# q and k of the first eight attention tiles loaded two tokens to a run and turned by products with the identity

## The chip, the cores and the metric

The kernel runs on one core of a Trainium2 chip. Its time is the device time of one execution: 847.76 us, the median of 3 runs (847.44 to 847.93). The core has a matrix engine (PE, with its weight loads PEld beside it), a vector engine (DVE), a scalar engine (ACT), GpSimd (POOL) and SyncE (SP), which here only issues DMAs.

## The reference

Three stages follow each other. Attention runs within chunks of 64 tokens: 4 batches x 8 heads x 576 tokens x 64. Its output, 2304 tokens x 512, goes through two layers of the same shape (512 to 2048 to 512) with different functions in the middle.

```python
scores = scale * np.matmul(q_c, k_c.transpose(0, 1, 2, 4, 3))   # 64 x 64 per chunk and head
scores = scores - np.max(scores, axis=-1, keepdims=True)
attn = np.exp(scores)
attn = attn / (np.sum(attn, axis=-1, keepdims=True) + 1e-09)
out = np.matmul(attn, v_c)
...
x = np.ascontiguousarray(attn_out.transpose(0, 2, 1, 3)).reshape(B * S, H * D)
h = x @ w_in                                                    # first layer
g = np.maximum(h, 0.0) + np.log1p(np.exp(-np.abs(h)))
x = g @ w_out
h = x @ w_in                                                    # second layer
g = P(h) / (Q(h) + 1e-6)                                        # two small polynomials
return g @ w_out
```

## The kernel before

**Tiles and blocks.** Attention works on 18 tiles of 128 tokens, two chunks each. The first layer takes tokens in blocks: three of 512 (blocks 0, 1, 2), then two of 384 that are computed as a pair. A block goes through 16 steps, one per 128 columns of the hidden layer. A step has 12 products `h` (L1065), two functions on ACT (`t` L1132 and `g` L1137), a subtraction on DVE that splits `g` in two parts (L1140), and 12 products `acc` (L1646). The 24 products of a step are 128x512. The second layer does the same with five blocks, the lines L1576 to L1608 and `acc` at L1679.

**Attention of a tile.** q and k are brought to a layout with the head dimension on the partitions (`qkT`), then come 16 products for the scores (L729, or L716), maximum, subtraction, exponential, sum and division on DVE and ACT (the division on POOL for tiles 7 to 17), the weights are turned (`aT`), 16 products with v (L857, or L845) follow, and the result is split into `xT`, an operand of the first layer.

**Two ways to turn.** The tiles in `STAGED` (0 to 6) turn q and k on PE, 4 transposes of 128x128 for q and 4 for k (`transpose`, L677), which ACT copies out of PSUM (`take`, L689); their attention weights are turned on PE too (L816, copied at L838). Tiles 7 to 17 turn on DVE, in blocks of 32x32: q and k at L701 and the weights in 8 instructions at L829. Their loads place such blocks where the DVE wants them, which takes 8 DMAs for q and 8 for k (`load_qk`, L618) and 4 for v (L633). A staged tile takes one DMA for q and one for k (L609; two where a batch ends inside the tile).

**What sets the order.** The kernel first lists tasks with an engine, a cost in us and what they read and write (`add`). A planner (`Program.schedule`) then simulates these costs with many random orders and keeps the one that ends first, and the program is written out in that order on every engine. For tiles 7 to 17 the planner counts 2.8 us for the q loads, 2.8 us for the k loads and 1.4 us for v. `BEGUN` and `BEGIN_AT` say how many tiles, and at which steps of blocks 0, 1 and 2, join the list of tasks. The wait for PE in the first microseconds is filled with products that compute nothing (`warm`, L1982).

**Buffers.** Loads of weights (`wr_1i`, `wr_2o`, ...) and of q and k of tiles 7 to 17 share 4 `raw` buffers. Weights arrive as 64-bit numbers and are put together in `cm_` tiles (3 buffers, tag `m`): ACT starts one (L468, L470), DVE finishes it (L474, L483). In blocks 1 and 2 the weights of the second layer are prepared in this way and stored back to DRAM (`store`, L523), and a `cm_` buffer is free when that store has landed. The results `h` have two PSUM buffers.

Of the kernel before, what the change touches and what calls it, by code (L numbers as in the profile page):

```python
# [11 lines left out]
F32 = mybir.dt.float32  # L12
# [8 lines left out]
P = 128  # L21
CH = 64
# [17 lines left out]
APART = (0, 3)  # L40
NP = 384
PIECES = ((0, 256), (256, 256))
STAGED = tuple(range(7))
LAST_FINISH = 12
LEAD = 0.0
LEAD2 = 0.0
BEGUN = (1, 5, 5)
BEGIN_AT = ((9,), (0, 3, 6, 9, 13), (0, 2, 4, 7, 9))
CONVERT = ((), (1, 2, 4, 5, 7, 8, 10, 11, 12, 14, 15), (1, 2, 3, 4, 5))
BACK = (0, 0, 1, *(1,) * 13)  # L50
QK_BY_VECTOR = {*range(18)} - {*STAGED}
# [251 lines left out]
def tile_chunk_attention_two_ffn(  # L303
# [276 lines left out]
    def attention(tb, scored_too=None):  # L580
# [14 lines left out]
        def chunks():  # L595
            for c in range(2):
                b, s = divmod(tb * TB + c * CH, S)
                yield c, b, s

        def load_qk(n):  # L600

            def f():
                if not staged and n == 0:
                    qk_t[tb] = raw.tile([P, 2, H, D], F32, tag="raw", name=f"qk_{tb}")
                if not qk_by_vector:
                    for off, m, b, s in runs(tb * TB, TB):
                        sync.dma_start(  # L609
                            out=qk_t[tb][off : off + m, n],  # L610
                            in_=(q, k)[n][b, :, s : s + m, :].rearrange("h p d -> p h d"),
                        )
                    return
                for c, b, s in chunks():
                    for d0 in range(0, D, 32):
                        for t0 in range(0, CH, 32):
                            p0 = CH * c + d0
                            sync.dma_start(  # L618
                                out=qk_t[tb][p0 : p0 + 32, n, :, t0 : t0 + 32],
                                in_=(q, k)[n][  # L620
                                    b, :, s + t0 : s + t0 + 32, d0 : d0 + 32
                                ].rearrange("h p d -> p h d"),
                            )

            return f

# [45 lines left out]
        def transpose(n):  # L672
            def f():
                if n == 0:
                    new_ps()
                for g in range(4):
                    pe.transpose(  # L677
                        bank(n)[:, g * P : (g + 1) * P],
                        qk_t[tb][:, n, 2 * g : 2 * g + 2].rearrange("p h d -> p (h d)"),
                        ident,  # L680
                    )

            return f

        def take(n):
            def f():
                if n == 0:
                    new_turned()
                act.activation(  # L689
                    tiles["qkT"][:, n].rearrange("p g t -> p (g t)"), bank(n), AF.Copy  # L690
                )

            return f
# [203 lines left out]
        km, ks = turn("mx", 4), turn("sm", 4)  # L897
        turned = [("turned", name, n) for n in range(16)]
        kr = [[(room_key[tb, n], h) for h in range(2)] if first else [] for n in range(2)]
        for n in range(2):  # L900
            loads["qk"[n], tb] = add(
                DMA, 2.8 if qk_by_vector else 1.2, load_qk(n), [],
                [(qkey, n)] if n else [qkey, (qkey, 0), (qkey, 1)],
                alloc=None if staged or n else "raw",
            )
        qks = [qkey, (qkey, 0), (qkey, 1)]
        if chained:

            def transposes():
                for n in range(2):  # L910
                    transpose(n)()

            begin[tb, 0] = add(PE, 0.9, transposes, qks, [b0, b1], alloc=alloc)
            for n in range(2):
                add(
                    ACT, 0.48, take(n), [(b0, b1)[n]], turned[8:] if n else turned,
                    alloc=None if n else "qkT",
                )
        elif not qk_by_vector:
            for n in range(2):  # L920
                begin[tb, n] = add(
                    PE, 0.46, transpose(n), [qkey, (qkey, n)], [(b0, b1)[n]] if n else [b0, b1],
                    alloc=None if n else alloc,
                )
                add(
                    ACT, 0.48, take(n), [(b0, b1)[n]],
                    turned[8 * n : 8 * n + 8] if n else turned + kr[0],
                    alloc=None if first or n else "qkT",
                )
        else:  # L930
            for n in range(2):
                add(
                    DVE, 0.6, turn_blocks(n), [qkey, (qkey, n)], turned[8:] if n else turned,
                    alloc=None if n else "qkT",
                )
        if not by_chunk:
# [3 lines left out]
        else:  # L940
            if not finish_attention(scores, turned):
                add(PE, 0.78, scores, turned, [b0, b1], alloc=alloc)
            add(DMA, 1.4, load_v, [], [(vkey, 0)], alloc="v")
        if scored_too:
            scored_too()
        if apart:
# [1012 lines left out]
    with tc.manual_schedule():  # L1959
# [2 lines left out]
        vec.memset(far_t, -FAR)  # L1962
        table(EXP_LN)
        for tb in STAGED:
            qk_t[tb] = wpool.tile([P, 2, H, D], F32, tag="wi", name=f"qk_{tb}")
        for fc in range(FC - len(STAGED)):
            wts[1, "i", fc] = new_w((1, "i", fc))
        for tb in STARTING:
# [59 lines left out]
```

## Time and profile before

| | us |
|---|---|
| median of 3 runs | 847.76 |
| the profiled execution | 849.12 |
| its span, first to last instruction | 847.3 |
| PE busy | 829.0 (98%) |
| DVE busy | 611.4 (72%) |
| ACT busy | 519.4 (61%) |
| POOL busy | 224.2 (26%) |

The profiled execution is 1.36 us above the median, and 1.82 us of it lie outside the span. A busy table gives for a stretch of the span each engine's busy time, the granted clock of PE as a share of 2.4 GHz, and the mean busy share of the 16 DMA engines. "x32" counts records; a product of two 4-byte operands (`warm`, scores, products with v) leaves two records, because PE goes over it twice, while a transpose leaves one.

### The profile page before, as it was taken

To read this page: it belongs to the slowest core of one execution; us is meant where nothing else is said; L and a number is where in the kernel's file an instruction comes from. 1 tells how busy PE (TensorE), PEld (TensorE's weight loads), DVE (VectorE), ACT (ScalarE), POOL (GpSimd) and SP (SyncE) were. 2 spreads that over 40 slices of the span, in tenths; PEclk is the share of its full clock that TensorE was granted. 3 is DMA by queue.
4 is the path that set the end of the run, shared out by engine and by line. 5 is a ranking of instruction groups with operands and counts; after the bars stand their busy time and mean duration, and the time that the engine had idled before them with its cause. 6 is when DMAs were issued, how large, how long until landed. Compare 5 with 4: busy or idle time off the path is not lost.

```text
span 847.3 us, 13413 instructions
## 1 busy us (share of the span) xinstructions
PE 829.0 (98%) x4978; PEld 706.7 (83%) x4978; DVE 611.4 (72%) x1080; ACT 519.4 (61%) x927; POOL 224.2 (26%) x205
## 2 busy tenths in 40 slices
PE   7999999999998899999999999999999999999998
PEld 6788878878877689999998888888889888888886
DVE  5778874675663668555379988778688886778775
ACT  5799863333321345555548788657678876667674
POOL 0000002242221241111111398332225262222131
PEclk9899999999999899999999999999999999999999
DMA  9975644655464101000383343010022000001001
GB/s 221 233 231 156 201 113 131 172 156 119 99 181 98 59 4 50 1 1 1 127 258 96 92 125 87 19 45 1 0 54 97 1 26 1 0 9 42 1 0 51
DMA packets 114722, 71.14 MB, mean 84 GB/s; under 512 B 84192, under 2 KB 102112, under 8 KB 114656
## 3 DMA queue, kind: packets, MB, share of 16 engines
q1 hardware_dynamic: 114656, 70.28, 30.4%
q8 instruction: 39, 0.64, 0.3%
q14 instruction: 27, 0.22, 0.1%
HBM read 56.63 MB, written 13.63 MB: 83 GB/s over the span
## 4 chain that ended last, share of the span: by engine, by line
PE 86%; DVE 4%; DMA 4%; ACT 2%; SPq 2%; issue 1%; POOL 0%; ACTq 0%; POOLq 0%; DVEq 0%
PE h L1065 34%; PE acc L1679 23%; PE acc L1646 20%; PE u L1453 3%; PE p L1453 3%; SPq L618 1%; DMA wr_1o<-in_moe_w_out_dram 1%; DMA wr_2i<-in_moe_w_in_dram 1%; PE warm L1982 1%; DMA qk<-in_k_dram 1%; DMA qk<-in_q_dram 1%; PE aps L845 1%; PE aps L677 1%; SPq L633 1%; DVE t L1553 0%
## 5 line engine op out<-in xcount | busy, mean ns | idle before, releaser
L1065 PE MATMUL h<-xT,w_2i 128*128 128x512 f32 (+1 forms) x960 | 208.7, 368 | 0.0
L1679 PE MATMUL acc<-w_2o,g 128*128 128x512 f32 x864 | 207.7, 390 | 0.1
L1065 PEld LDWEIGHTS h<-xT,w_2i 128*128 128x128 f32 x960 | 169.0, 188 | 31.4 <-ACT u L1576 0.3
L1679 PEld LDWEIGHTS acc<-w_2o,g 128*128 128x128 f32 x864 | 161.1, 188 | 33.7 <-POOL g L1583 0.9
L1646 PE MATMUL acc<-g,w_1o 128*128 128x512 f32 (+1 forms) x768 | 177.9, 378 | 1.6 <-ACT g L1137 0.8
L1646 PEld LDWEIGHTS acc<-g,w_1o 128*128 128x128 f32 x768 | 140.5, 188 | 25.0 <-DVE g L1140 1.5
L1583 POOL TENSOR_TENSOR g<-t,g 128x512 fp32r<-128x512 f32 (+1 forms) x80 | 95.5, 1195 | 232.4 <-ACT g L1580 181.0
L1065 PE MATMUL h<-xT,w_1i 128*128 128x512 f32 x564 | 137.4, 395 | 7.3 <-ACT g L1137 7.3
L1065 PEld LDWEIGHTS h<-xT,w_1i 128*128 128x128 f32 x564 | 106.3, 190 | 30.6 <-ACT g L1137 8.3
L1608 DVE TENSOR_TENSOR t<-h,t 128x512 f32<-128x512 f32 (+1 forms) x80 | 50.9, 636 | 31.8 <-ACT t L1568 12.9
L1597 ACT ACTIVATE t<-h,row 128x512 f32<-128x512 f32 (+1 forms) x80 | 58.7, 733 | 24.3 <-PE h L1065 23.8
L1140 POOL TENSOR_TENSOR g<-t,g 128x512 fp32r<-128x512 f32 x32 | 43.2, 1350 | 103.0 <-ACT g L1137 101.8
L1553 DVE SCALAR_TENSOR_TENSOR t<-t,row,u 128x512 f32<-128x512 f32 (+1 forms) x80 | 55.2, 691 | 19.6 <-ACT u L1576 19.0
L1572 ACT ACTIVATE u<-t,row 128x512 f32<-128x512 f32 (+1 forms) x80 | 51.8, 648 | 25.0 <-DVE t L1553 24.3
L1553 DVE SCALAR_TENSOR_TENSOR t<-t,row,h 128x512 f32<-128x512 f32 (+1 forms) x80 | 55.3, 692 | 12.9 <-ACT u L1550 5.7
L1580 ACT ACTIVATE g<-t 128x512 fp32r<-128x512 f32 (+1 forms) x80 | 46.8, 585 | 27.6 <-DVE t L1553 23.7
L1568 ACT ACTIVATE t<-h,row 128x512 f32<-128x512 f32 (+1 forms) x80 | 51.2, 642 | 17.1 <-PE h L1065 9.8
L1553 DVE SCALAR_TENSOR_TENSOR t<-u,row,t 128x512 f32<-128x512 f32 (+1 forms) x80 | 55.3, 693 | 6.0 <-ACT u L1550 5.8
L1553 DVE SCALAR_TENSOR_TENSOR u<-t,row,u 128x512 f32<-128x512 f32 (+1 forms) x80 | 55.5, 695 | 0.0
L1132 ACT ACTIVATE t<-h 128x512 f32<-128x512 f32 x48 | 28.4, 594 | 42.7 <-PE h L1065 41.8
L809 POOL TENSOR_TENSOR e<-e,sm 128x512 f32<-128x512 f32 x11 | 12.6, 1144 | 152.6 <-DVE sm L805 147.9
L1550 ACT ACTIVATE u<-h 128x512 f32<-128x512 f32 (+1 forms) x80 | 43.3, 542 | 14.9 <-DVE t L1608 9.7
(157 smaller groups left out, 1037.3 us busy)
## 6 DMA issues: line engine op xcount, KB each, us to landing
wr_1i<-in_moe_w_in_dram SPq DMA_DIRECT2D x16, 512.0 KB, 5.0
wr_1o<-in_moe_w_out_dram SPq DMA_DIRECT2D x16, 512.0 KB, 5.0
wr_2i<-in_moe_w_in_dram SPq DMA_DIRECT2D x16, 512.0 KB, 4.7
wr_2o<-in_moe_w_out_dram SPq DMA_DIRECT2D x16, 512.0 KB, 5.1
out_dram<-ev SPq DMA_DIRECT2D x16, 256.0 KB, 2.1
x<-ev SPq DMA_DIRECT2D x6, 512.0 KB, 2.7
x2r<-x SPq DMA_DIRECT2D x6, 512.0 KB, 4.6
qk<-in_q_dram SPq DMA_DIRECT2D x88, 32.0 KB, 3.0
```

What stands on the lines that cost most here:

```text
L1065: pe.matmul(hs[s], w[:, a, c * P : (c + 1) * P], xt[:, b, c, :n_tok], start=n == 0, stop=n == 3 * KC - 1,)
L1453: pe.matmul(banks[n], lhs(a, i, c), right(b, j, c), start=start and m == 0, stop=m == 5, skip_group_check=not start,)
L1550: act.activation(u(), h(), AF.Square)
L1553: return lambda: vec.scalar_tensor_tensor(out=out(), in0=in0(), scalar=scalar, in1=in1(), op0=op0, op1=op1)
L1568: act.activation(new("t1"), h(), AF.Abs, scale=b_t[:, 0:1])
L1572: act.activation(u(), d(), AF.Ln, bias=epsq_t)
L1580: act.activation(gs[s][:, 0, :n_tok], p(), AF.Copy)
L1583: pool.tensor_tensor(out=gs[s][:, 1, :n_tok], in0=p(), in1=gs[s][:, 0, :n_tok].bitcast(F32), op=ALU.subtract,)
L1597: lambda: act.activation(new("t2"), h(), AF.Identity, scale=na_t[:, 3:4], bias=na_t[:, 2:3]),
L1608: lambda: vec.tensor_tensor(out=p(), in0=h(), in1=p(), op=ALU.mult), [hkey, kp], [kp],
L1646: pe.matmul(accs[1, j, half][c % 2][:, :n_tok], wts[1, "o", fc][:, a, c * P : (c + 1) * P], gs[s][:, b, :n_tok], start=first and n == 0, s ...
L1679: pe.matmul(accs[2, j, half][c % 2], gs[s][:, b, c * P : (c + 1) * P], wts[2, "o", fc][:, a, :], start=first and n == 0, stop=last and n == 2,
```

## The change

Tile 7 becomes a staged tile, so that eight tiles turn q and k on PE. A staged tile now keeps q on partitions 0 to 63 and k on 64 to 127, with two neighbouring tokens of a head side by side: runs of 512 bytes in DRAM where runs of 256 bytes were read. Since a partition holds two tokens, the 4 + 4 transposes become 8 products for the even tokens and 8 for the odd ones: 128 rows by 64 columns of data stand in PE, the identity's 128 columns pass through, and the results go by turns to the lower and the upper half of the PSUM partitions. Both sets need q and k. ACT's copy out of PSUM puts even and odd tokens back in order.

For the other ten tiles the 16 DMAs of q and k stay as they are, but are listed as eight tasks of two DMAs at 0.95 us each; v counts 2.0 us. Five tiles joined the list in block 1 and five in block 2, one in block 0; now six and four, and none in block 0.

```diff
-STAGED = tuple(range(7))
+STAGED = tuple(range(8))
...
-BEGUN = (1, 5, 5)
-BEGIN_AT = ((9,), (0, 3, 6, 9, 13), (0, 2, 4, 7, 9))
+BEGUN = (0, 6, 4)
+BEGIN_AT = ((), (0, 3, 6, 9, 11, 14), (0, 3, 6, 9))
...
+        def load_part(n, c, d0):
+            def f():
+                if (n, c, d0) == (0, 0, 0):
+                    qk_t[tb] = raw.tile([P, 2, H, D], F32, tag="raw", name=f"qk_{tb}")
+                b, s = divmod(tb * TB + c * CH, S)
+                p0 = CH * c + d0
+                for t0 in range(0, CH, 32):
+                    sync.dma_start(
+                        out=qk_t[tb][p0 : p0 + 32, n, :, t0 : t0 + 32],
+                        in_=(q, k)[n][b, :, s + t0 : s + t0 + 32, d0 : d0 + 32].rearrange(
+                            "h p d -> p h d"
+                        ),
+                    )
...
         def load_qk(n):
...
+                for off, m, b, s in runs(tb * TB, TB):
+                    p0 = CH * n + off // 2
+                    sync.dma_start(
+                        out=qk_t[tb][p0 : p0 + m // 2].rearrange("p h t d -> p h (t d)"),
+                        in_=(q, k)[n][b, :, s : s + m, :].rearrange(
+                            "h (p t) d -> p h (t d)", t=2
+                        ),
+                    )
...
-                for g in range(4):
-                    pe.transpose(
-                        bank(n)[:, g * P : (g + 1) * P],
-                        qk_t[tb][:, n, 2 * g : 2 * g + 2].rearrange("p h d -> p (h d)"),
-                        ident,
+                for h in range(H):
+                    p0, col = 64 * (h % 2), h // 2 * P
+                    pe.matmul(
+                        bank(n)[p0 : p0 + 64, col : col + P], qk_t[tb][:, h, n], ident,
+                        start=True, stop=True,
                     )
...
                 act.activation(
-                    tiles["qkT"][:, n].rearrange("p g t -> p (g t)"), bank(n), AF.Copy
+                    tiles["qkT"].rearrange("p n g (u t) -> p t g n u", t=2)[:, n],
+                    bank(n).rearrange("p (g n u) -> p g n u", g=4, n=2),
+                    AF.Copy,
                 )
...
-            loads["qk"[n], tb] = add(
-                DMA, 2.8 if qk_by_vector else 1.2, load_qk(n), [],
-                [(qkey, n)] if n else [qkey, (qkey, 0), (qkey, 1)],
-                alloc=None if staged or n else "raw",
-            )
+            if staged:
+                loads["qk"[n], tb] = add(
+                    DMA, 1.0, load_qk(n), [], [(qkey, n)] if n else [qkey, (qkey, 0), (qkey, 1)]
+                )
+                continue
+            for part_key in loaded_parts[n]:
+                begins = part_key == loaded_parts[0][0]
+                loads["qk"[n], tb] = add(
+                    DMA, 0.95, load_part(*part_key[1:]), [],
+                    [qkey, *loaded_parts[0], *loaded_parts[1]] if begins else [part_key],
+                    alloc="raw" if begins else None,
+                )
...
-                    PE, 0.46, transpose(n), [qkey, (qkey, n)], [(b0, b1)[n]] if n else [b0, b1],
+                    PE, 0.46, transpose(n), qks, [(b0, b1)[n]] if n else [b0, b1],
...
-            add(DMA, 1.4, load_v, [], [(vkey, 0)], alloc="v")
+            add(DMA, 2.0, load_v, [], [(vkey, 0)], alloc="v")
```

The order of the program changes on every engine, since the planner starts anew. Three places follow, before and then after. Names end in a running number that grows with the place in the program.

**SyncE in the middle of block 2.** Before: the last two tiles' loads (`qk_2803`, `qk_2860`) and the stores `w2o` and `w2i` of prepared weights.

```order
L618 DMA qk_2803<-in_q_dram 32x8x32 x8
L618 DMA qk_2803<-in_k_dram 32x8x32 x8
L618 DMA qk_2860<-in_q_dram 32x8x32 x8
L633 DMA v_2912<-in_v_dram 64x4x64 x4
L618 DMA qk_2860<-in_k_dram 32x8x32 x8
L523 DMA w2o_2959<-cm_2o_2528 128x512
L523 DMA w2i_2967<-cm_2i_2683 128x512
```

After, the same place, with the last two tiles `qk_2883` and `qk_2989`:

```order
L607 DMA qk_2883<-in_q_dram 32x8x32 x6
L607 DMA qk_2883<-in_k_dram 32x8x32 x2
L607 DMA qk_2883<-in_q_dram 32x8x32 x2
L607 DMA qk_2883<-in_k_dram 32x8x32 x6
L638 DMA v_2958<-in_v_dram 64x4x64 x4
L523 DMA w2i_2985<-cm_2i_2728 128x512
L607 DMA qk_2989<-in_q_dram 32x8x32 x4
L607 DMA qk_2989<-in_k_dram 32x8x32 x2
L607 DMA qk_2989<-in_q_dram 32x8x32 x4
L607 DMA qk_2989<-in_k_dram 32x8x32 x6
L523 DMA w2o_3083<-cm_2o_2878 128x512
L523 DMA w2o_3087<-cm_2o_2665 128x512
```

One store has moved between the two tiles' loads, and v of the first of them stands between them as well; the store of the oldest `cm_` tile (`cm_2o_2665`; before `cm_2o_2528`) still stands behind both tiles.

**ACT at the same place.** Before, from the function `t` of step 39 on:

```order
L1132 ACTIVATE t_39_2955<-h_39_2917 128x512
L1137 ACTIVATE g_2985<-h_39_2917 128x512
L470 ACTIVATE cm_2i_2993<-wr_2i_2776 128x512
L470 ACTIVATE cm_2o_2997<-wr_2o_2791 128x512
L1132 ACTIVATE t_40_3014<-h_40_2972 128x512
L1132 ACTIVATE t_41_3026<-h_41_3000 128x512
L1137 ACTIVATE g_3071<-h_40_2972 128x512
```

After, from `t` of step 39 on:

```order
L1147 ACTIVATE t_39_2999<-h_39_2966 128x512
L1147 ACTIVATE t_40_3057<-h_40_3004 128x512
L1152 ACTIVATE g_3081<-h_39_2966 128x512
L781 ACTIVATE e_3071<-e_3071,row 128x512
L1152 ACTIVATE g_3119<-h_40_3004 128x512
L470 ACTIVATE cm_2i_3124<-wr_2i_2841 128x512
L470 ACTIVATE cm_2o_3127<-wr_2o_2844 128x512
L1051 ACTIVATE xb_3137<-aps 128x512
L1147 ACTIVATE t_41_3140<-h_41_3105 128x512
L1152 ACTIVATE g_3167<-h_41_3105 128x512
```

Before, the two conversions `cm_2i` and `cm_2o`, which take the buffers that the stores free, stand ahead of `t` and `g` of step 40. After, they stand behind both, and ahead of `t` and `g` of step 41.

**PE where the first step begins.** Before, from the turned weights of tile 1 on (`room_1_132`; 134 and 136 are tiles 2 and 3):

```order
L816 MATMUL aps_173<-ident,room_1_132 128x128 x4
L816 MATMUL aps_208<-ident,room_1_134 128x128 x4
L857 MATMUL aps_173<-room_1_132,v_138 64x64 x16
L857 MATMUL aps_208<-room_1_134,v_139 64x64 x16
L1982 MATMUL warm_407<-ident 128x128 x2
L816 MATMUL aps_0_245<-ident,room_1_136 128x128 x4
L1982 MATMUL warm_407<-ident 128x128
L1090 MATMUL h_0_421<-xT_330,w_1i_120 128x256 x4
```

After:

```order
L823 MATMUL aps_198<-ident,room_1_132 128x128 x4
L864 MATMUL aps_198<-room_1_132,v_138 64x64 x16
L823 MATMUL aps_222<-ident,room_1_134 128x128 x4
L823 MATMUL aps_0_262<-ident,room_1_136 128x128 x4
L864 MATMUL aps_222<-room_1_134,v_139 64x64 x16
L1105 MATMUL h_0_446<-xT_363,w_1i_121 128x256 x4
```

The `warm` products between the tiles are gone, and so is their place ahead of the turned weights of tile 3.

## Rows read from the trace of the kernel before

**Rows 1.** part 1 of the page: busy us (share of the span) xinstructions
```profile
PE 829.0 (98%) x4978; PEld 706.7 (83%) x4978; DVE 611.4 (72%) x1080; ACT 519.4 (61%) x927; POOL 224.2 (26%) x205
```

**Rows 2.** busy table, 300 to 400 us: length, engines, clock, DMA share, GB/s
```profile
300.00:400.00 100.00, 100.00 (x575) 95.66 (x574) 66.23 (x135) 52.84 (x116) 21.51 (x21) 1.00 0.03 11
```

**Rows 3.** the waits of PE: us in total, times, longest
```profile
PE h L1065 <- ACT g L1137: 7.3, 3, 6.0
```

**Rows 4.** PE in time order, 262 to 285 us: start, us, what [idle]
```profile
263.40 5.60 PE L1065 MATMUL h<-xT,w_1i 128*128 128x512 f32 x24
...
278.86 4.69 PE L1065 MATMUL h<-xT,w_1i 128*128 128x512 f32 x12 [6.04 <-ACT g L1137]
```

**Rows 5.** ACT in order of time, 225 to 300 us
```profile
276.08 0.66 ACT L470 ACTIVATE cm_2i<-wr_2i 128x512 f32<-128x512 f32 x1 [11.82 <-DMA w2o<-cm_2o]
```

**Rows 6.** SyncE's DMA issues in order of time, 100 to 310 us
```profile
251.13 5.29 SPq L618 DMA_DIRECT2D qk<-in_q_dram  x8
...
261.52 3.85 SPq L618 DMA_DIRECT2D qk<-in_q_dram  x8
265.47 2.58 SPq L633 DMA_DIRECT2D v<-in_v_dram  x4
268.09 4.06 SPq L618 DMA_DIRECT2D qk<-in_k_dram  x8
272.19 0.46 SPq L523 DMA_DIRECT2D w2o<-cm_2o  x1
```

**Rows 7.** chain that ended last, 40 to 62 us: start, us, what
```profile
48.06 0.62 PE aps L857 x32
48.68 0.47 PE aps L729 x32
...
58.90 0.44 PE aps L816 x4
...
60.74 0.87 PE aps L677 x8
```

**Rows 8.** the same chain, 0 to 120 us
```profile
6.55 0.45 PE warm L1982 x4
```

**Rows 9.** PE in order of time, 60 to 300 us
```profile
109.62 4.15 PE L1646 MATMUL acc<-g,w_1o 128*128 128x512 f32 x17 [0.58 <-DVE g L1140]
```

**Rows 10.** busy table, three stretches of the start
```profile
2.00:12.00 10.00, 9.81 (x119) 8.80 (x118) 2.99 (x7) 4.12 (x8) 0.00 (x0) 1.00 1.27 223
...
22.00:24.00 2.00, 1.71 (x8) 1.71 (x9) 1.99 (x5) 1.07 (x3) 0.00 (x0) 0.50 1.25 261
...
45.00:50.00 5.00, 5.00 (x83) 4.00 (x82) 3.59 (x7) 4.97 (x9) 0.00 (x0) 1.00 1.04 362
```

**Rows 11.** DVE in order of time, 0 to 50 us
```profile
8.19 0.76 DVE L754 TENSOR_REDUCE mx<-aps 128x4 f32<-128x256 f32 x2 [7.29 <-PE aps L729]
...
10.42 0.69 DVE L754 TENSOR_REDUCE mx<-aps 128x8 f32<-128x512 f32 x1 [0.82 <-PE aps L729]
...
12.65 0.69 DVE L809 TENSOR_TENSOR room<-room,sm 128x512 f32<-128x512 f32 x1
```

**Rows 12.** PE in order of time, 0 to 60 us
```profile
18.38 1.26 PE L816 MATMUL aps<-ident,room 128*128 128x128 f32 x8 [2.84 <-DVE room L809]
...
22.30 1.22 PE L1982 MATMUL warm<-ident 128*128 128x128 f32 x4 [0.59 <-DVE xT L415]
...
24.45 1.20 PE L1090 MATMUL h<-xT,w_1i 128*128 128x256 f32 x4
```

**Rows 13.** ACT by line, 24 to 112 us: count, busy, mean ns, idle
```profile
L370 ACT ACT_TABLE_LOAD x18 | 23.1, 1283 | 0.3
...
L689 ACT ACTIVATE qkT<-aps 128x512 f32<-128x512 f32 x6 | 3.6, 603 | 1.0 <-PE aps L677 1.0
```

**Rows 14.** busy table, 40 to 112 us
```profile
40.00:80.00 40.00, 39.66 (x333) 32.13 (x333) 32.37 (x61) 38.62 (x60) 0.00 (x0) 1.00 0.61 174
80.00:112.00 32.00, 31.42 (x167) 25.34 (x166) 27.89 (x52) 28.06 (x41) 1.04 (x1) 1.00 0.71 223
```

More of the change, by code (lines that the diff above doesn't have):

```diff
@@ L598, in chunks @@
                 yield c, b, s
+        def load_part(n, c, d0):
[11 more added lines that the diff above has]
+                    )
+            return f
         def load_qk(n):
             def f():
[L605 to L611, printed above, removed]
-                        )
[L613 to L623, printed above, removed]
+                for off, m, b, s in runs(tb * TB, TB):
[6 more added lines that the diff above has]
+                    )
             return f
@@ L899, in attention @@
         kr = [[(room_key[tb, n], h) for h in range(2)] if first else [] for n in range(2)]
+        loaded_parts = [[(qkey, n, c, d0) for c in range(2) for d0 in (0, 32)] for n in range(2)]
         for n in range(2):
-            loads["qk"[n], tb] = add(
-                DMA, 2.8 if qk_by_vector else 1.2, load_qk(n), [],
-                [(qkey, n)] if n else [qkey, (qkey, 0), (qkey, 1)],
-                alloc=None if staged or n else "raw",
-            )
+            if staged:
[10 more added lines that the diff above has]
+                )
         qks = [qkey, (qkey, 0), (qkey, 1)]
@@ L932, in attention @@
                 add(
-                    DVE, 0.6, turn_blocks(n), [qkey, (qkey, n)], turned[8:] if n else turned,
+                    DVE, 0.6, turn_blocks(n), [qkey, *loaded_parts[n]], turned[8:] if n else turned,
                     alloc=None if n else "qkT",
@@ L1964, in tile_chunk_attention_two_ffn @@
         for tb in STAGED:
-            qk_t[tb] = wpool.tile([P, 2, H, D], F32, tag="wi", name=f"qk_{tb}")
+            qk_t[tb] = wpool.tile([P, H, 2, D], F32, tag="wi", name=f"qk_{tb}")
         for fc in range(FC - len(STAGED)):
```

## The prediction

> **What bounds the kernel now.** I read the busy times first: PE works 829.0 of 847.3 us [rows 1]. Then the busy table by stretches: behind 300 us PE has no gap to give back [rows 2], so whatever this change wins or loses is won or lost in the first 300 us, and every microsecond of work added to PE there shows in full unless it falls into a gap. Third, the waits of PE: 7.3 us in three waits for one function of ACT [rows 3]. In order of time, 6.04 us of it is a single gap in block 2, and the 12 products behind it took 4.69 us, while 24 took 5.60 just before [rows 4]; beside 5.60 / 2 = 2.8 that is 1.9 us more, since PE came back at the lower clock. The place costs 7.9 us. Fourth, what ACT waited for there: 11.82 us ahead of a conversion of weights, for a store of an older tile [rows 5]. Fifth, why the store was late: SyncE issued the q and k loads of two tiles and a v load ahead of it [rows 6], 21.1 us from the first (251.13) to the store (272.19). So this wait is a queue on SyncE, not a lack of bandwidth. The rest of the gaps are small, apart from the start, where PE waits for the tiles' softmax on DVE.
>
> **The change part by part.** The sum is made against the profiled execution, 849.12 us, which is 1.36 us above the median 847.76; I carry the difference over to the median.
>
> *The queue of block 2.* One tile's 16 loads of q and k take SyncE 3.85 + 4.06 = 7.9 us, and v 2.58 [rows 6], 10.5 together. The planner counted 2.8 + 2.8 + 1.4 = 7.0, so behind two tiles and one v it took the stores for 2 x 2.3 + 1.2 = 5.8 us earlier than they were. It now counts 8 x 0.95 + 2.0 = 9.6. In the new order the oldest conversion tile's store still stands behind two tiles' loads, so SyncE needs some 2 x 7.9 + 2.58 + a store = 19 us there, not much less than 21.1. What differs is who is queued behind the wait: on ACT the two conversions moved from ahead of the functions of step 40 to behind them. PE then has a further step of 24 products (2 x 2.8 = 5.6 us, by the products of [rows 4]) plus the scores and values of a tile (0.47 + 0.62 [rows 7]) = 6.7 us before it needs what ACT holds back. That covers the 6.04 us even if the stores come as late as before, and SyncE has 2 us less to do. Term: -7.9. If the loads start later than before by more than about 2.7 us (6.7 - 6.04 + 2), the difference comes back; bounds -7.9 and 0.
>
> *Turning on PE.* A transposed tile costs 0.87 us in 8 transposes [rows 7]. The new 16 products pass 128 columns over PE twice. The nearest row by columns is the warm product: 0.45 us for four passes, 0.11 each [rows 8]. One after another 32 passes are 3.6 us; if the lower and the upper half run side by side, 1.8. Products on a part of the array do overlap in this trace: the scores make 32 passes of half as many columns, 32 x 0.056 = 1.8 us one by one, in 0.47 us, 3.8 at a time; those with v in 0.62, 2.9 at a time [rows 7]. Four at a time cannot come from different rows of the array alone, so two column halves can run together. With v, where neighbours in the queue change the column half first, as here, each 32 passes cost 0.62 - 1.8/4 = 0.17 us above the ideal; 1.8 + 0.17 gives 2.0 us per tile, the value I take, between 1.8 and 3.6. Tiles 4, 5 and 6 lie on PE's full stretch: 3 x (2.0 - 0.87) = +3.4 (2.8 to 8.2). Tile 7 had cost PE nothing for turning; now 2.0 for q and k and 0.44 for its weights [rows 7]: +2.4 (2.2 to 4.0).
>
> The Trainium skill ("TensorE: Matmul & The Clock Gate", Part 3, What overlaps and what doesn't) says that a weight load overlaps products in flight only when it goes to another row group. Here all products use all rows, so by that rule each of the loads would stand bare. By it the price would lie towards the upper bound above; the scores row, in which two column halves share rows, speaks against the strict reading, and no row shows 128 rows by 64 columns.
>
> *Relief on DVE.* Tile 7 loses two transposes and eight small ones on DVE at about 100 us, where PE waited 0.58 us for DVE [rows 9]. Term: -0.6, between -0.6 and 0.
>
> *The start.* Tiles 0 to 3 also turn with 2.0 instead of 0.87 us, in a stretch where PE waits for data anyway: in 2 to 12 us the loads came at 223 GB/s with the DMA engines full [rows 10]. In 45 to 50 us, with weights in longer runs under way, it was 362 GB/s [rows 10]; 512-byte runs lie between, and if a packet has a fixed cost, they give 1 / (1/362 + (1/223 - 1/362)/2) = 276 GB/s. Four tiles' q and k are 2.1 MB: 9.4 us before, 7.6 us after, so the last tile's data is some 1.8 us earlier (0 to 3.6). But nothing can be turned now before k has come. Behind k's arrival stood 0.44 us of turning and now stand 2.0; a quarter of the 1.8 us is won, so tile 0's scores come 2.0 - 0.44 - 0.45 = 1.1 us later, and DVE begins at 9.3 instead of 8.19 [rows 11]. The scores of tile 1 stand behind the turning of tiles 1 and 2: 9.3 + 4.0 + 0.5 = 13.8 instead of 10.42. Until then DVE can finish the sum and the division of tile 0, 0.69 each by the row of the division [rows 11], which came later before: 3.4 - 1.4 = 2 us later in all. Against it: the weights of tiles 1 and 2 were turned after a gap of 2.84 us, then two warm products held PE, 0.59 us of waiting and 1.22 of work at the clock 0.50, ahead of tile 3, and the first step began at 24.45 [rows 10, 12]. Those two are gone in the new order. Two later, two earlier: term 0, between -2 (the clock holds, since the gap is shorter) and +6 (four tiles at 3.6 us: (3.6 - 2.0) x 4 = 6.4).
>
> *ACT and the loads in block 0.* ACT gets three copies more (two of q and k, one of the weights, 0.60 each) and two table loads more in block 0 (1.28 each [rows 13]): 4.4 us. It was busy 38.62 of 40 us up to 80 and 28.06 of 32 up to 112 [rows 14], so 5.3 us were free, and PE's 5.8 us of added work lengthen the block as much. Tile 7's loads are earlier too, into the time of full DMA. I take +0.5 for new short waits, between 0 and 3. The interleaved order of ACT's copy has no row; at the double of 0.60 it would be 0.6 x 16 = 9.6 us of ACT work, of which four tiles lie in the block; the data is read in runs of 64, so I count nothing.
>
> Sum: -7.9 + 3.4 + 2.4 - 0.6 + 0 + 0.5 = -2.2. The profiled execution would take 846.9, the median 847.76 - 2.2 = 845.6 us.
>
> **The rivals.** *The two halves do not run side by side* (slower). Place: the 16 products of each staged tile. At 3.6 us a tile, tiles 4 to 7 cost 8.2 + 3.2 + 0.4 = 11.8 us instead of 5.8, and the first step starts 6 us later: 845.6 + 6.0 + 6.0 = 857.6. The scores row speaks against it. The change turns to a loss where a tile costs more than 2.0 + 2.2 / 4 = 2.55 us even with an unchanged start.
>
> *The wait of block 2 stays or comes back elsewhere* (slower). Ten tiles still pass SyncE in two blocks, six of them in block 1, which had five; a late store again holds ACT. For it: the oldest store stands behind two tiles as before. Against: the planner's costs now fit the measured ones to 10%. With three quarters of the 7.9 us lost, 845.6 + 6 = 851.6.
>
> *A better start.* Loads at over 300 GB/s and PE's clock held at the start: the first step 2 to 4 us earlier, 845.6 - 3 = 842.6. For it: 362 GB/s, and the clock at 0.50 just before the first step [rows 10]. Against: DVE is the engine that is full there. A page of the Trainium skill ("SBUF — State Buffer", Door 1: The DMA port swizzle) says that partitions 0 to 63 reach only half of the ports; as q goes to that half alone, this would leave the loads at their old rate and the case out. No row shows a load of 64 partitions by itself.
>
> **How the numbers follow.** Forecast 0.55, its own range 842.5 to 849. Halves one by one 0.14, the wait of block 2 0.13, a better start 0.18. A change below 0.2%, 1.7 us, cannot be told from none by this measurement. Below 846.1: the better start (0.18) and six tenths of the forecast (0.33): 0.51. Within 846.1 to 849.5: the rest of the forecast, 0.22. Above: the two slower cases, 0.27. The range 841 to 853 leaves out the halves one by one and a tail of the better start.
>
> **What would show it.** The 16 products of a tile take 1.8 to 2.2 us in the chain. PE has no gap over 2 us in block 2, ACT no wait over 8 us ahead of a conversion, and the clock stays at 1.00 from 30 us on. The first 512-column step starts at 30 us, as before. PE's busy time rises by about 5 us, less the warm products that are gone. The forecast is wrong if a tile costs over 2.5 us on PE, or if a gap of over 3 us stands anywhere between 40 and 300 us.

## The result, and the profile after

The changed kernel took 854.37 us (median of four runs, 853.10 to 857.96) beside 847.60 for the kernel before on the same chip (847.36 to 847.93): 1.0082 times as long, interval 1.0065 to 1.0099. The forecast was 845.6, and the range ended at 853. The change made the kernel slower by some 7 us.

Part 1 of the page of the profiled execution (854.56 us, span 852.8) answers to [rows 1]: PE is busy for 6.5 us more, the span is 5.5 longer.

```profile
PE 835.5 (98%) x5166; PEld 713.4 (84%) x5166; DVE 605.6 (71%) x1070; ACT 524.2 (61%) x932; POOL 221.9 (26%) x205
```

The busy table (length, PE, weight loads, DVE, ACT, POOL, clock, DMA share, GB/s) in 260 to 300 us, where the kernel before had its gap of 6.04 us [rows 4]: PE is busy throughout and the clock is 1.00. The wait of block 2 is gone, as forecast. In 300 to 400 us PE is busy throughout as well, as in [rows 2]. The conversion of the accumulator that ends block 2 begins at 328.69, before at 322.54, and the span ends 5.5 us later: the loss is made ahead of it.

```profile
260.00:300.00 40.00, 40.00 (x353) 32.68 (x352) 26.50 (x50) 13.45 (x24) 12.36 (x11) 1.00 0.42 99
300.00:400.00 100.00, 100.00 (x567) 94.77 (x566) 67.42 (x133) 52.04 (x114) 21.99 (x21) 1.00 0.03 11
```

How it went can be seen on SyncE and ACT (in order of time, against [rows 5, 6]). From the first load of the last two tiles to the two `w2o` stores, the second of them that of the oldest `cm_` tile, SyncE took 24.8 us, where it had taken 21.1 before. So the store came no earlier; but of ACT's two conversions, now behind the functions of step 40, one stood 0.61 us for a store and the other not at all, where 11.82 had been.

```profile
258.06 3.25 SPq L607 DMA_DIRECT2D qk<-in_q_dram  x6
...
282.83 0.92 SPq L523 DMA_DIRECT2D w2o<-cm_2o  x2
```

```profile
285.02 0.68 ACT L470 ACTIVATE cm_2o<-wr_2o 128x512 f32<-128x512 f32 x1 [0.61 <-DMA w2o<-cm_2o]
```

The waits of PE in 40 to 300 us (us in total, times, longest) are to be held against [rows 3]: there is still one long wait for the function of ACT.

```profile
PE h L1080 <- ACT g L1152: 4.4, 1, 4.4
PE h L1080 <- ACT w_1i L407: 1.2, 1, 1.2
```

PE in order of time, 205 to 236 us, shows where it now stands: at 227, the end of block 1. The 12 products behind it took 5.49 us and the next 12 3.23, where 12 take 2.88 in the last row; in 227 to 232 us the clock's row is 0.50. With the gap that is 4.39 + 2.61 + 0.35 = 7.35 us, about what the wait of block 2 had cost.

```profile
213.23 0.69 PE L852 MATMUL aps<-aT,v 64*64 64x64 f32 x32
...
214.32 3.02 PE L1661 MATMUL acc<-g,w_1o 128*128 128x512 f32 x12
217.18 5.60 PE L1080 MATMUL h<-xT,w_1i 128*128 128x512 f32 x24
227.17 5.49 PE L1080 MATMUL h<-xT,w_1i 128*128 128x512 f32 x12 [4.39 <-ACT g L1152]
232.46 3.23 PE L1661 MATMUL acc<-g,w_1o 128*128 128x512 f32 x12
235.53 2.88 PE L1080 MATMUL h<-xT,w_1i 128*128 128x512 f32 x12
```

ACT in the same stretch answers to [rows 5]. It is no store that holds it this time: the conversion of an attention tile's result (L407, `xT`) stood for 7.52 us and began 0.04 us after PE's 24 products ended (217.18 + 5.60 = 222.78). Its data had been on hand since 214. Behind it came an exponential that waited for DVE, and only then the functions `t` and `g` for which PE stood still.

```profile
222.82 0.60 ACT L407 ACTIVATE xT<-aps 128x512 fp32r<-128x512 f32 x1 [7.52 <-PE h L1080]
225.43 0.72 ACT L781 ACTIVATE e<-e,row 128x512 f32<-128x512 f32 x1 [2.01 <-DVE e L771]
226.06 0.58 ACT L1147 ACTIVATE t<-h 128x512 f32<-128x512 f32 x1
226.53 1.07 ACT L1152 ACTIVATE g<-h 128x512 fp32r<-128x512 f32 x2
```

The order of ACT has it as a row ahead of those functions (without numbers):

```
L407 ACTIVATE xT_2469<-aps 128x4x128
L781 ACTIVATE e_2486<-e_2486,row 128x512
L1147 ACTIVATE t_30_2526<-h_30_2491 128x512
L1152 ACTIVATE g_2530<-h_30_2491 128x512
```

Why did it wait for those products? Block 3's operand `xT_3` is the fourth of a pool of two buffers (`xpool`), so it takes that of block 1, which the products of steps 30 and 31 still read. Tile 12, the first of block 3, now begins in block 1 at `fc` 11 (the number of the step in its block), and its finish is added when tile 13 begins, at `fc` 14, in the loop ahead of the products of that step (step 30 of the whole) and the next. The planner knows a buffer's readers from the tasks added so far, so it knows nothing of these two steps' reads and puts the conversion ahead of the functions of step 30. Before, tile 13 began in block 2.

The start, PE in order of time, answers to [rows 8, 12]. The first turn waits 1.66 us for k and begins at 5.95; the first 512-column step begins at 33.04 (before: 30.04, the row below these, +3.0).

```profile
5.95 1.97 PE L683 MATMUL aps<-ident,qk 128*64 128x128 f32 x32 [1.66 <-DMA qk<-in_k_dram]
7.84 0.94 PE L1997 MATMUL warm<-ident 128*128 128x128 f32 x6
8.71 0.69 PE L736 MATMUL aps<-room 64*64 64x64 f32 x32
9.33 3.71 PE L683 MATMUL aps<-ident,qk 128*64 128x128 f32 x64
...
20.95 0.66 PE L823 MATMUL aps<-ident,room 128*128 128x128 f32 x4 [1.68 <-DVE room L816]
...
26.32 1.22 PE L1105 MATMUL h<-xT,w_1i 128*128 128x256 f32 x4
...
30.56 1.97 PE L683 MATMUL aps<-ident,qk 128*64 128x128 f32 x32
...
33.04 2.91 PE L1080 MATMUL h<-xT,w_1i 128*128 128x512 f32 x12
```

```profile
30.04 2.91 PE L1065 MATMUL h<-xT,w_1i 128*128 128x512 f32 x12
```

A turn is 32 records in 1.97 us, and two tiles in a row take 3.71: about 1.9 us each, so the two halves do run side by side. DVE in order of time answers to [rows 11]: it meets tile 0 at 9.53 (8.19 before) and tile 1 at 13.74 (10.42), much as the prediction had them.

```profile
9.53 0.42 DVE L761 TENSOR_REDUCE mx<-aps 128x4 f32<-128x256 f32 x1 [8.63 <-PE aps L736]
...
13.74 0.69 DVE L761 TENSOR_REDUCE mx<-aps 128x8 f32<-128x512 f32 x1
```

The busy table, two stretches of the start, answers to [rows 10]: the loads came at 208 GB/s, no faster than the 223 before, where 276 had been estimated, and at 22 us the clock is 0.50 once more.

```profile
2.00:12.00 10.00, 8.34 (x129) 7.72 (x130) 1.61 (x4) 1.95 (x5) 0.00 (x0) 1.00 1.15 208
22.00:24.00 2.00, 1.70 (x35) 1.59 (x36) 2.00 (x9) 1.43 (x3) 0.00 (x0) 0.50 0.95 318
```

Last, ACT by line, 24 to 112 us (count, busy, mean ns, idle): the interleaved copy takes 633 ns beside the 603 of [rows 13]. It is as good as free.

```profile
L694 ACT ACTIVATE qkT<-aps 128x512 f32<-128x512 f32 x8 | 5.1, 633 | 1.6 <-PE aps L683 1.6
```

### The profile page after: what moved, and what is told of

It reads as the page before. It is cut to its first block, busy times and chain, and to the rows that moved or that the text cites. A ratio compares the mean times of both kernels' runs of the same rounds, so it can differ in the third digit from the quotient of the medians.

```text
span 852.8 us, 13697 instructions
## 1 busy us (share of the span) xinstructions
PE 835.5 (98%) x5166; PEld 713.4 (84%) x5166; DVE 605.6 (71%) x1070; ACT 524.2 (61%) x932; POOL 221.9 (26%) x205
## 4 chain that ended last, share of the span: by engine, by line
PE 90%; DVE 3%; ACT 2%; DMA 2%; issue 1%; POOL 1%; SPq 0%; DVEq 0%; ACTq 0%; POOLq 0%
PE h L1080 36%; PE acc L1661 23%; PE acc L1694 20%; PE u L1468 3%; PE p L1468 3%; PE aps L683 2%; DVE t L1568 1%; DMA wr_1o<-in_moe_w_out_dram 1%; PE aps L852 1%; PE aps L864 1%; PE aps L723 1%; DMA qk<-in_k_dram 1%; PE aps L823 0%; PE aps L736 0%; PE h L1105 0%
## 5 line engine op out<-in xcount | busy, mean ns | idle before, releaser
L1152 ACT ACTIVATE g<-h 128x512 fp32r<-128x512 f32 x48 | 28.5, 598 | 45.0 <-PE acc L1661 44.9
```

## The experiments

Theory: the change is a gain (the wait of block 2) and three losses: the wait for block 1's operand buffer, the price of the products, and loads onto 64 partitions that are no faster. Rivals: the new wait is again a late transfer on SyncE; the start is late by the order of the work alone. Every ratio is to the kernel before, run on the same chip in the same turn (its medians there: 848.09 for experiments 1 to 4, 849.01 for 5 to 8, 847.93 for 9 and 10). The planner draws its order anew wherever its costs or `BEGUN` change, so the kernels with (0, 6, 4) and the new items share one order, those with (0, 5, 5) another, and experiments 5 and 6 have one each.

**1. The conversion of tile 12 later.** Of the order made by the planner, tasks 734 to 751 without 736 (the conversion, and tile 13's softmax behind it) are put behind the function of step 31.

```diff
-        for i, t in prog.schedule():
+        plan = prog.schedule()
+        late = [p for p in plan if 734 <= p[0] <= 751 and p[0] != 736]
+        plan = [p for p in plan if p not in late]
+        n = [i for i, t in plan].index(773) + 1
+        plan[n:n] = late
+        for i, t in plan:
```

> The changed kernel with one thing moved: the conversion of tile 12's result into the operand buffer of block 3, and what follows it for tile 13 (maximum, shift, exponential, sum, division, turning), stand on ACT, DVE and POOL behind the two functions of step 31 and no longer ahead of those of step 30. My theory: block 3's operand takes the buffer that block 1's products read until step 31, so ACT stood 7.52 us before a buffer that only those products could free, and the functions that PE needed next stood behind it. Then PE's gap of 4.39 us at 227 and the lower clock behind it go (together 7.35 us): 847.0 us, between 846 and 849. Rival: ACT was late because of weights that came late over SyncE; then the gap stays over 3 us in another place and the time is 852 to 855.

Measured: 853.18 (849.32 to 857.82), 1.0056 (1.0035 to 1.0077). The gap at the end of block 1 is gone, as its busy table shows for 210 to 235 us (in the changed kernel PE was busy for 20.61 us of that, at a clock of 0.86), and block 1 took 94.1 us from the first conversion of an accumulator to the next, not 101.1.

```profile
210.00:235.00 25.00, 25.00 (x168) 20.19 (x167) 13.77 (x27) 8.03 (x14) 4.88 (x4) 1.00 0.59 145
```

But most of the time did not come back. The waits of PE in 25 to 300 us name a new one: the softmax that was moved holds the turning of the next tile on DVE (2.0 us at 243, and the clock was 0.97 in 235 to 300).

```profile
PE h L1080 <- ACT w_1i L407: 2.4, 1, 2.4
PE aps L723 <- DVE qkT L708: 2.0, 1, 2.0
PE h L1080 <- ACT g L1152: 1.7, 1, 1.7
```

The other two stand in block 0, which this edit doesn't touch; they are longer than in the changed kernel's profile (1.21 and 0.65), and this profile was of the longest of the nine runs. The place is shown, the size of 7 us isn't; for that see experiments 8 and 9.

**2. Turned as before, in the changed order.** 256-byte runs onto 128 partitions and 8 transposes a tile; eight tiles staged, load items and order of the changed kernel.

```diff
...
-                for h in range(H):
-                    p0, col = 64 * (h % 2), h // 2 * P
-                    pe.matmul(
-                        bank(n)[p0 : p0 + 64, col : col + P], qk_t[tb][:, h, n], ident,
-                        start=True, stop=True,
+                for g in range(4):
+                    pe.transpose(
+                        bank(n)[:, g * P : (g + 1) * P],
+                        qk_t[tb][:, n, 2 * g : 2 * g + 2].rearrange("p h d -> p (h d)"),
+                        ident,
...
```

> The changed kernel with q and k of the eight tiles loaded in 256-byte runs onto 128 partitions and turned by transposes again, all else in the changed order. My theory: the changed order has no part in the late start. Then tiles 4 to 7 give back 4 x (1.9 - 0.87) = 4.1 us and the start 3.0 us: 854.4 - 7.1 = 847.3; the first 512-column step starts at 30 us and the gap at 227 stays. Rival: the start is late by the order in which DVE and PE take tiles 0 to 3; then only 4.1 us come back, 850.3, and the first 512-column step starts after 32 us.

Measured: 849.05 (846.42 to 850.00), 1.0004 (0.9990 to 1.0017), 0.78% or 6.6 us below the changed kernel's ratio. The first 512-column step began at 29.91 and the gap at the end of block 1 stayed 4.39. The time lies between the theory's 847.3 and the rival's 850.3; the step at 29.91 decides for the theory. So the start was not late by its order.

**3. Products, but the old runs.** Only the loads are as before; the 16 products read `qk_t[tb][:, n, h]`.

> The changed kernel with 256-byte runs onto 128 partitions, but still 16 products with the identity for each tile. It parts the start in two. If the start is late because a product needs both q and k and the loads onto 64 partitions are no faster, the first product starts at 4.1 us and about 1 to 1.5 us come back: 853. If it is late by the price of the products alone, nothing comes back: 854.4. If the loads onto 64 partitions were slower, 2 us or more: 852 or less, and the rate of 2 to 14 us rises to 216 to 240 GB/s.

Measured: 853.18 (850.84 to 853.80), 1.0050 (1.0029 to 1.0071). The first turn began at 4.22, without a wait, but took 2.81 us, and the first 512-column step began at 33.82. The loads came at 224 GB/s in 2 to 12 us, as in the kernel before (214 in 2 to 14). So with the products the start is late even when the loads are as before; the intervals of this run and the changed kernel's overlap, and experiment 9 gives the sizes.

**4. q on even, k on odd partitions.** Still 512-byte runs, still 64 partitions a load, but spread over all 128.

```diff
-                    p0 = CH * n + off // 2
+                    p0 = off + n
...
-                        out=qk_t[tb][p0 : p0 + m // 2].rearrange("p h t d -> p h (t d)"),
+                        out=qk_t[tb][p0 : off + m : 2].rearrange("p h t d -> p h (t d)"),
...
-                    bank(n).rearrange("p (g n u) -> p g n u", g=4, n=2),
+                    bank(n).rearrange("p (g u n) -> p g n u", g=4, n=2),
```

> The changed kernel with q on the even and k on the odd partitions, still in 512-byte runs: each load now reaches over all 128 partitions. Theory of the port (64 neighbouring partitions reach only a part of the DMA's way into SBUF): the rate in 2 to 14 us rises from 208 to about 276 GB/s, the last of the four tiles' data is 1.5 to 2 us earlier and the first 512-column step starts at 31 to 32 us: 852.5 to 853.5. Rival: something else sets the rate (packets' own cost, HBM); then it stays at 203 to 213 GB/s and the time at 854.4.

Measured: 852.11 (849.25 to 853.09), 1.0039 (1.0023 to 1.0055). The busy table, 2 to 12 us, has the loads at 259 GB/s (265 in 2 to 14), where the changed kernel's came at 208; the first turn began at 5.08, the first 512-column step at 30.76. The ten runs fall into two groups, three at 849.3 to 849.5, the profiled one among them, and seven at 851.7 to 853.1; the profile shows the quicker group.

```profile
2.00:12.00 10.00, 9.21 (x145) 8.52 (x144) 1.60 (x4) 2.81 (x6) 0.00 (x0) 1.00 1.03 259
```

The bytes, the runs and the number of partitions are the same; only which partitions they are differs. So the place of the 64 partitions set the rate.

**5. The load items alone** in the kernel before (eight of 0.95 and v at 2.0; seven tiles staged, transposes, 1 + 5 + 5 tiles).

> The kernel before with the load items alone: q and k of a tile behind the first seven in eight items of 0.95 each and v at 2.0, all else as before (seven staged tiles, transposes, 1 + 5 + 5 tiles begun in the blocks). Theory that the planner's counting was the cause of the wait in block 2 (my prediction's first term): PE's gap of 6.04 us at 279 and the lower clock behind it are gone, 848 - 7.9 = 840. Rival: the wait went because block 2 has four tiles to begin and no longer five; then a gap of 4 us or more stays in 240 to 300 us and the time is 847 to 849.

Measured: 847.20 (845.01 to 849.90), 0.9980 (0.9968 to 0.9991). Block 2's gap is gone with its five tiles still there: from the first conversion of an accumulator to the next it took 92.2 us, not 99.4. PE has no gap over 0.3 us in 240 to 300 us. The time is the rival's, 847, without the rival's wait: the new order has a gap of its own in block 0, as PE in order of time shows, where ACT stood 3.34 us for weights ahead of a load of its table:

```profile
41.04 5.49 PE L1089 MATMUL h<-xT,w_1i 128*128 128x512 f32 x12 [6.43 <-ACT g L1161]
```

**6. The old items** in the changed kernel (one of 2.8 for q and one for k, v at 1.4).

> The changed kernel with the load items of before (q and k one item each of 2.8, v 1.4), all else changed: eight staged tiles, products, 0 + 6 + 4 tiles. Counting theory: the wait in block 2 comes back (a gap of 4 to 6 us in 240 to 300 us) beside the one at the end of block 1, which has nothing to do with the loads: 854 + 6 = 860. Rival (four tiles in block 2 are enough): no gap over 2 us there, 854. In both ACT's conversion of tile 12 stands ahead of the functions of step 30 in this order too, so a gap of 4 us at the end of block 1 stays.

Measured: 872.31 (871.79 to 873.00), 1.0271 (1.0254 to 1.0288): worse than both theories had it. PE waits 16.4 us for the function of ACT, in four gaps: 5.52 at 205 (ACT had stood 7.88 us for a load of weights), 4.39 at 236 (the operand buffer, 11.24 on ACT), 1.04 at 269 and 5.43 at 293. SyncE's issues ahead of the last show the queue of [rows 6] once more, and ACT in order of time what stood behind it:

```profile
272.09 4.15 SPq L607 DMA_DIRECT2D qk<-in_k_dram  x8
276.34 2.58 SPq L643 DMA_DIRECT2D v<-in_v_dram  x4
279.03 3.99 SPq L607 DMA_DIRECT2D qk<-in_q_dram  x8
283.07 5.18 SPq L607 DMA_DIRECT2D qk<-in_k_dram  x8
288.29 0.45 SPq L523 DMA_DIRECT2D w2o<-cm_2o  x1
```

```profile
290.53 0.66 ACT L470 ACTIVATE cm_2i<-wr_2i 128x512 f32<-128x512 f32 x1 [7.25 <-DMA w2o<-cm_2o]
```

So four tiles in block 2 are not enough without the new counting, and by 5 five tiles do no harm with it. The wait for a late store stands in both orders made with the old counting (before, and here) and in none of the three made with the new (the changed kernel, 5, and that of 7 to 10). It is the counting of the loads, not the number of tiles in block 2, that removed the wait.

**7. Even and odd partitions, five tiles in each block.** As 4, with tile 13 begun in block 2, so that tile 12 is finished behind block 1's last products:

```diff
-BEGUN = (0, 6, 4)
-BEGIN_AT = ((), (0, 3, 6, 9, 11, 14), (0, 3, 6, 9))
+BEGUN = (0, 5, 5)
+BEGIN_AT = ((), (0, 3, 6, 9, 12), (0, 2, 4, 7, 9))
```

> The changed kernel with q on the even and k on the odd partitions, and with five tiles begun in block 1 and five in block 2 (so tile 12 is finished behind block 1's last step). Theory: PE's gap of 4.4 us at the end of block 1 and the clock lost behind it go, as ACT's conversion of tile 12 now stands behind the functions of steps 30 and 31: 852.1 - 7 = 845. Rival: with five tiles in block 2 the late stores come back there, a gap of 3 us or more in 250 to 300 us: 850.

Measured: 847.41 (845.07 to 848.16), 0.9979 (0.9970 to 0.9988). PE has no gap over 0.15 us in 40 to 300 us. The first 512-column step, though, began at 34.15: the first turn took 3.68 us. The time missed both expectations.

**8. Turned as before, five tiles in each block.** As 2, with the edit of 7.

> As the run with 256-byte runs and transposes in the changed order (849.05), but with five tiles begun in block 1 and five in block 2. Theory: the 4.39 us at the end of block 1 go with the clock behind them, 849.0 - 7 = 842, which would be faster than both kernels. Rival: a late store in block 2 takes its place, 846 to 849.

Measured: 840.88 (840.73 to 842.11), 0.9906 (0.9892 to 0.9921): faster than both kernels. Beside experiment 2 the buffer's wait is worth 0.98%, 8.3 us. PE's waits in 28 to 300 us are one:

```profile
PE h L1080 <- ACT g L1152: 1.9, 1, 1.9
```

**9. The changed kernel with five tiles in each block, and the same with the old runs.** The edit of 7 alone; and that with the loads of 3, so that it differs from 8 by the products alone.

> The changed kernel with five tiles begun in block 1 and five in block 2 and nothing else edited. Theory: the 4.39 us at the end of block 1 and the clock lost behind it (7.35 us together) go, the late start and the dearer turning stay: 854.4 - 7.4 = 847. Rival: with five tiles begun in block 2 a late store holds ACT there again, a gap over 3 us in 250 to 300 us, 850 or more.

> Five tiles in each block, 256-byte runs onto 128 partitions, but the 16 products in place of the 8 transposes; beside the run with transposes (840.9) the products alone differ. Theory: tiles 4 to 7 cost 4 x 1.0 = 4.1 more, and the start, where four tiles are turned before the last of them can go to DVE, 3 to 4 more: 848 to 849. Rival: the price of a turn hides behind the loads and DVE at the start, 845.

Measured: 848.49 (847.50 to 848.76), 1.0011 (1.0001 to 1.0020); and 845.59 (844.34 to 846.42), 0.9972 (0.9961 to 0.9982). In the first kernel, the changed one with five tiles in each block, PE waits once between 28 and 300 us, for 0.65 us, so no late store took the wait's place. The steps between these runs (8, the second, the first, the changed kernel) give the account: wait 0.71% (1.0082 to 1.0011), 6.0 us; runs onto 64 partitions 0.39%, 3.3 us; products 0.66%, 5.6 us, of which tiles 4 to 7 have 4 x (1.9 - 0.87) = 4.1. By the intervals each step is good to some 1.5 us, and the runs stand in three turns; the step of the wait holds all else that the other order changes. The other way, with six and four tiles until the last step (changed kernel, 3, 2, 8), they are 2.7 for the runs, 3.9 for the products, and 8.3 for the wait. The first 512-column step, 29.62 with transposes (8), 32.65 with products and old runs, came at 35.21 in the changed layout. The expectation for the products, 848 to 849, was too high, and the rival's number, 845, came out, though not in its way: the start is 3.0 us later. But PE's order of time in 8 has a wait at 35 us and 4.61 us for 12 products behind it, of which the later start leaves a wait of 0.58 and 3.01 us. So in the profiles nearly all of the 3.0 us came back, and the spans, 844.1 and 840.3, differ by 3.8; the 5.6 of the medians holds 1.5 us more than tiles 4 to 7 explain.

```profile
35.00 4.61 PE L1080 MATMUL h<-xT,w_1i 128*128 128x512 f32 x12 [1.85 <-ACT g L1152]
```

**10. More warm products ahead of the first turn**, 10 where there were 6 in the first kernel of 9 (`WARM` 2.3 and not 1.4), and 9 in that of 7 (2.0).

> As the run before with 10 warm products ahead of the first tile where there were 6, so that PE does not stand still while it waits for k of tile 0. Theory: the first turn takes 1.97 us in some runs and 3.4 to 3.7 in others because PE stood still before it; with PE at work it takes 1.9, the first 512-column step starts at 33 us or earlier, and the times scatter by less than 2 us; the median is 0.5 to 1 below that of the run with 6. Rival: the wait has no part in it; then the first turn still takes over 3 us in this profile, or time and scatter are those of the run with 6.

> Even and odd partitions, five tiles in each block, and 9 warm products where there were 6. In the run with 6 the first turn took 3.68 us, each record 421 ns and not 272, and the first 512-column step started at 34.15 (in the changed order 30.76, with a first turn of 1.97). Theory: with PE at work until k comes the turn takes 1.9 and the step starts at 31 to 32.5: 847.4 - 2 = 845.4. Rival: nothing changes, 847.

Measured: 848.10 (847.05 to 854.28), 1.0006 (0.9988 to 1.0023); and 845.74 (844.83 to 847.01), 0.9975 (0.9964 to 0.9987). In the first, PE in order of time begins the turn at 6.05 with no wait named:

```profile
6.05 1.97 PE L683 MATMUL aps<-ident,qk 128*64 128x128 f32 x32
```

In the first kernel of 9, with 6 warm products, the same view has

```profile
5.93 3.68 PE L683 MATMUL aps<-ident,qk 128*64 128x128 f32 x32 [1.64 <-DMA qk<-in_k_dram]
```

So the turn is 1.7 us shorter, and the first 512-column step came 2.0 us earlier (33.16). With even and odd partitions the turn took 2.41 and the step began at 32.99, not 34.15. The time of the whole did not follow by a size that these intervals can tell (1.0011 to 1.0006; 0.9979 to 0.9975): in the first kernel a wait of 1.50 us at 48 us took most of it back. Nine of its runs lie within 1.4 us, as those of 9 do, but one took 854.28, so the theory that the first turn makes the scatter fell; what does is open. In both the turn was shorter with more work ahead of it. But a wait just before it does not alone decide: the turn took 2.81 us in experiment 3 and 3.17 in the second kernel of 9, both without a wait, and 1.97 in the changed kernel behind a wait of 1.66. The last section has what fits all of them.

## Why the prediction was wrong

*The queue of block 2: right.* Taken as -7.9. With what else is not the products, the layout or the buffer (DVE's relief, ACT's short waits, tile 7's 0.87 + 0.44 on PE) the prediction had -7.9 - 0.6 + 0.5 + 1.3 = -6.7; experiment 8 has -0.94%, -8.0 us. Its mechanism holds: the oldest store came as late as before, even later (24.8 us behind the first load, where the prediction had some 19), and did no harm, since the conversions stood behind the functions of step 40. That the new counting of SyncE's time brought such an order is what experiments 5 and 6 show. The two small terms, -0.6 and +0.5, all but cancel, and PE's short waits from 28 to 130 us do add up to 1.9 us in either profile.

*"A late store again holds ACT": the step that failed.* For a new wait the sum had nothing. Six tiles in block 1 were named, with 851.6 and a chance of 0.13, but with the wrong mechanism: the argument against it, that the counted costs now fit, is true and bears on SyncE alone. The prediction looked for the next wait only in the queue in which the old one had stood. That the sixth tile is one of block 3, whose operand needs block 1's buffer, could be read from `xpool`'s two buffers and from the order of ACT, where `xT_2469` stands ahead of `t_30`. It cost 6.0 us (experiment 9) to 8.3 (8 beside 2), 7.35 by the profile. The prediction had named its own sign: a gap of over 3 us between 40 and 300 us, and 4.39 stood there.

*Turning on PE: right.* 2.0 us a tile were taken, 1.9 measured; products that load 128 rows by 64 columns do run two at a time. The Trainium skill ("TensorE: Matmul & The Clock Gate", Part 3, What overlaps and what doesn't) lets a weight load overlap only where the row group differs; here all products share all rows, and the trace does not agree with its strict reading: two tiles took 3.71 us, where their 64 weight loads, 137 ns each in the trace, would take 8.8 one after another.

*The start: the term of 0 was mis-sized.* The delays on PE and DVE were about right (1.1 later for tile 0: 1.34; tile 1 at 13.8: 13.74), the gain was not: the loads came at 208 GB/s, not above the 223 of before, and the clock was 0.50 in 22 to 24 us as before. Measured: +3.0 for the first 512-column step in this profile, and 5.6 + 3.3 - 4.1 = 4.8 us of time (3.9 + 2.7 - 4.1 = 2.5 the other way) that the products and the layout cost beyond tiles 4 to 7, where the term had 0 and its bound +6. The estimate of 276 GB/s for 512-byte runs was good for runs spread over all partitions (259 to 263 in 2 to 12 us, 265 to 270 in 2 to 14); onto 64 neighbours it was 196 to 208. The Trainium skill ("SBUF — State Buffer", Door 1: The DMA port swizzle) says that partitions 0 to 63 reach one half of the ports; experiment 4 agrees, since even partitions reach both halves and the rate rose by a quarter. The prediction used that rule only to argue against a gain, as a weight on a rival; it should have stood in the term.

*The sum.* Forecast: -6.7 for all that is not the products, 4.5 for them on tiles 4 to 7, 0 at the start, 0 for a new wait: -2.2. Measured, by the steps between the runs: -8.0, then 5.6 + 3.3 = 8.9 for products and layout, then 6.0 for the buffer (or 6.6 and 8.3): 6.9. That these steps add up to the 0.82% of the result is no proof of them, since they are differences along one chain of kernels.

## What to carry to other kernels

When a change moves work forward past a block's end, ask which buffer the moved work writes and who still reads it: in a pool of two the wait can be for products that come later on another engine, and whatever stands behind the waiting instruction in its queue pays. A planner that learns a buffer's readers as tasks are added cannot see the readers added later. Here a longer run bought DMA rate only where its destination was spread over the partitions, and even then no time: with five tiles in each block 512-byte runs on even and odd partitions (0.9979, experiment 7) were no better than the old runs (0.9972, 9). A layout that spares a transfer can cost more on the engine that must undo it.

## What the chip showed that was not expected

At the start the same 32 products of a first turn took 1.97 us in three profiles, 2.41 to 3.17 in three and 3.39 to 3.68 in four, and the clock's row says 1.00 in all. It says so for want of a record: the profile's records of the granted clock begin only at 4.4 to 10.2 us, and a stretch without one is counted as 1.00. In all 14 profiles the time of a product of 128 columns falls from 421 ns to some 273 at about that moment, or, where PE then stood still, when it goes on. In the kernel before, where it is 5.98 us, four records of `warm` take

```profile
5.05 1.06 PE L1982 MATMUL warm<-ident 128*128 128x128 f32 x4
...
6.39 0.61 PE L1982 MATMUL warm<-ident 128*128 128x128 f32 x4
```

and 1.22 at the recorded 0.50 of [rows 10, 12]. So PE ran at the lower level until then, and a first turn is long as far as it lies ahead of that moment. In the eight profiles in which PE worked on without a wait until then, it came at 5.0 to 6.7 us. In four of the six with a wait for k it came at 8.9 to 10.2 us, in the other two, the changed kernel and experiment 4, at 4.4 and 4.6, just as the wait began. Why those two differ is open.

64 partitions taken as every second one received 259 to 263 GB/s of 512-byte runs in 2 to 12 us, as neighbours 196 to 208, with equal runs and bytes; the old 256-byte runs onto all 128 came at 220 to 224.
